# First transforms in four 64x64 tiles, x's rows spread over 128 partitions, and a new order of SP's transfers

## The chip, the cores and the metric

The kernel runs on one core of a Trainium2 chip. The metric is device microseconds (us) of one execution. Engines are named as the profile names them: PE (TensorE's matmuls), PEld (its weight loads), DVE (VectorE), ACT (ScalarE), POOL (GpSimd) and SP (SyncE, which here only issues transfers).

## What is computed

A spectral layer and two dense layers on a batch of two sequences, 3008 positions by 256 features, in float32:

```python
X = np.fft.rfft(x, axis=1)                   # x: (2, 3008, 256)
Yr = Xr @ w_r - Xi @ w_i + b_r               # 256 x 256, complex
Yi = Xr @ w_i + Xi @ w_r + b_i
Yr, Yi = soft_threshold(Yr, 0.01), soft_threshold(Yi, 0.01)
y = np.fft.irfft(Yr + 1j * Yi, n=3008, axis=1)
h = y.reshape(6016, 256) @ w_in1             # to 2048, leaky slope alpha, back to 256
z = leaky(h, alpha) @ w_out1
out = smooth_relu(z @ w_in2) @ w_out2        # the same shapes again
```

## The kernel before

The transform of length 3008 is split as 47 x 64. The work comes in this order.

- **f1**, the first transform, along 47 points. `x` is prepared on the host as 16 groups (8 of each of the two batches) of 96 rows: 48 rows (47 and a row of zeros) of one half of the 64 points and 48 of the other, 4 KB a row. `load_x(g)` brings a group to partitions 0 to 95 of a tile of its own, `f1(g)` multiplies it with the 96x96 constant `c47` in four matmuls of 256 columns (float32, which the trace shows as two instructions each) into two banks, ACT copies one bank and DVE the other to the tile `ae`, and `store_a(g, h)` writes `ae` to DRAM: h=0 the rows for frequencies 0 to 11, from 48 partitions, h=1 those for 12 to 23 from the other 48.
- **f2**, the second transform, works on 24 items (12 of each batch), each two of the 24 frequencies k. `load_a(b, parts)` brings k ranges of the stored intermediate to the tile `a` of batch b with 128 partitions; `A_PARTS` are the pairs (first k, number of k). Item i reads k = 2i and 2i+1, a piece of the constants `m`, and later of `n` (`load_mn`).
- Behind f2 come `mix` (the complex 256x256 product with the weights `wm`), the threshold, `i1` (first inverse transform, its result `ve` stored to DRAM by `v_dr<-ve`, two items a transfer, through two buffers in turn), `load_v` and `p3` (the last transform: 48 rows on each half of the partitions, products of 64 rows by 64 columns on the four quarters of PE). The loop over items runs f2 of item j+2, mix of item j and i1 of item j-2 in turn, and beside them the conversion of the first dense layer's weights (`load_w` brings `u`; ACT begins each with the line that reads `u`).
- The two dense layers follow, from about 150 us to the end.

The order is written out by hand: engines run their instructions in the order of the code. Nearly all transfers are issued by SP, in one queue. SP's and ACT's transfers share eight completion semaphores in turn, so that a transfer also waits for the one that used its semaphore last. A transfer that must wait (for an evicted tile, or a store that it reads) holds up all behind it on SP. PE likewise waits in order: where f2 of an item has no data, nothing behind it runs.

Of the kernel before, what the change touches and what calls it, by code (L numbers as in the profile page):

```python
# [31 lines left out]
def fourier_constants():  # L32

    import numpy as np

    n1, k1 = np.arange(R1), np.arange(NK)
    a = 2 * np.pi * (np.outer(n1, k1) % R1) / R1

    c = np.zeros((2, 48, 2, 2, NK))
    for par in range(2):  # L40
        c[par, :R1, 0, par] = np.cos(a)
        c[par, :R1, 1, par] = -np.sin(a)
    c = c.reshape(96, 4, 2, NK // 2).transpose(0, 2, 1, 3).reshape(96, 96)
# [51 lines left out]
def spectral_mlp_kernel(ctx: ExitStack, tc: tile.TileContext, x, w_r, w_i, bias, c_f1, c_f2,  # L95
                        c_i1, c_i2, w_in1, w_out1, alpha, w_in2, w_out2, out):
    nc = tc.nc
    V, A, G, T = nc.vector, nc.scalar, nc.gpsimd, nc.tensor
# [3 lines left out]
    psum = ctx.enter_context(tc.tile_pool(name="psum", bufs=2, space=PSUM))  # L102
# [19 lines left out]
    def block(tag, shape, dtype, name):  # L122
        return base.tile(shape, dtype, tag=tag, name=name)
# [6 lines left out]
        p = block(f"p{npiece[0] % NP}", [128, 1024], F32R, name)  # L130
        return p[:, 112:112 + 768]

    a_dr = [[dram.tile([NT, 48, D], F32, name=f"a_dr{b}_{h}") for h in range(2)] for b in range(B)]
    v_dr = [dram.tile([96, NT, D], F32, name=f"v_dr{b}") for b in range(B)]


# [199 lines left out]
    def obank(shape, name, ahead=None):  # L336
# [14 lines left out]
    xs = {}

    def load_x(g):
        b, j = divmod(g, 8)
        tag = f"p{g}" if g < 6 else f"w{g - 6}" if g < 14 else f"c{g - 12}"
        xs[g] = block(tag, [96, 4, D], F32, f"x{b}_{j}")
        if g == 0:
            nc.sync.dma_start(xs[g][:, 0:1, :], x[b, j, :, 0:1, :])
            nc.sync.dma_start(xs[g][:, 1:4, :], x[b, j, :, 1:4, :])
        else:  # L360
            nc.sync.dma_start(xs[g], x[b, j])

    A_PARTS = ((0, 2), (2, 2), (4, 2), (6, 2), (8, 4), (12, 6), (18, 6))

    def load_a(b, parts):
        if a_sb[b] is None:
            a_sb[b] = block(f"a{b}", [128, NK, D], F32, f"a_{b}")
        for k, n in parts:
            h, k0 = divmod(k, NK // 2)
            src = a_dr[b][h].rearrange("t (q k) f -> (t q) k f", q=4)  # L370
            nc.sync.dma_start(a_sb[b][:, k:k + n, :], src[:, k0:k0 + n, :])

    def store_a(g, h):
        b, j = divmod(g, 8)
        nc.sync.dma_start(a_dr[b][h][4 * j:4 * j + 4].rearrange("t p f -> p t f"), aes[g][48 * h:48 * h + 48])

    def load_mn(k, tiles, src, h=None):

        s = slice(0, 8) if h is None else slice(4 * h, 4 * h + 4)
        nc.sync.dma_start(tiles[k][:, s, :].rearrange("p k f -> p (k f)"),  # L380
                          src[:, 1024 * k + 128 * s.start:1024 * k + 128 * s.stop])
# [3 lines left out]
    def f1(g):  # L385
        b, j = divmod(g, 8)
        if g < 10:
            ae = block(f"w{8 + g}" if g < 5 else f"m{1 + g}" if g < 8 else f"w{g - 8}", [96, 4, D], F32, f"ae{g}")
        else:
            if g == 10:  # L390
                late.append(block("a1", [96, 6, 4, D], F32, "ae_late"))
            ae = late[0][:, g - 10]
        aes[g] = ae
        for i in range(2):
            ps = psum.tile([96, 2, D], F32, tag="h" if i else "e", name=f"ps1_{b}_{j}_{i}")
            for u in range(2):
                T.matmul(ps[:, u, :], c47, xs[g][:, 2 * i + u, :], start=True, stop=True)
            if i == 0:
                A.activation(ae[:, 0:2, :], ps, AF.Copy)
            else:  # L400
                V.tensor_copy(ae[:, 2:4, :], ps)
# [16 lines left out]
    for g in range(8):  # L418
        f1(g)
        store_a(g, 0)  # L420
        load_x(8 + g)
        if g == 3:
            load_mn(0, m_t, c_f2, 0)
        if g in (1, 2):
            A.dma_start(wm32[g - 1], (w_r, w_i)[g - 1].rearrange("(c p) e -> p c e", p=128))
    load_a(0, A_PARTS[:2])
    load_mn(0, m_t, c_f2, 1)
    load_a(0, A_PARTS[2:5])
    load_mn(1, m_t, c_f2, 0)
    load_mn(0, n_t, c_i1, 0)  # L430
    for g in range(8):
        store_a(g, 1)
    load_mn(1, m_t, c_f2, 1)
    load_mn(0, n_t, c_i1, 1)
    load_a(0, A_PARTS[5:])
    load_mn(1, n_t, c_i1)
    load_mn(2, m_t, c_f2)
# [54 lines left out]
    def split_wm(k, w):  # L492
        hi, lo = (wm[k][:, z].rearrange("p c (h q) -> p c q h", h=2) for z in range(2))
        split(w.rearrange("p c (q h) -> p c q h", h=2), hi, lo, A)

    for g in range(8, 16):
        f1(g)
        if g < 15:
            store_a(g, 0)
        if g == 8:  # L500
            T.matmul(ri[0].rearrange("p z e -> p (z e)"), ones, b_t[0:1].rearrange("p z e -> p (z e)"), start=True, stop=True)
            V.tensor_copy(b_t, ri[0])
        if g == 9:
            split_wm(0, wm32[0])
            V.scalar_tensor_tensor(ws[0], wm32[0], -1.0, wm32[1], op0=ALU.mult, op1=ALU.subtract)
        if g == 11:
            split_wm(1, ws[0])
            V.tensor_tensor(ws[1], wm32[1], wm32[0], op=ALU.subtract)
        if g == 13:
            split_wm(2, ws[1])  # L510
# [169 lines left out]
            ops[int(what[0])](what[1])  # L680
    for name in "HshLl":
        ops[2](name)
    store_a(15, 0)
    for j in range(n):
        parts = f2_parts(*items[j + 2]) if 0 < j < n - 2 else None
        if j + 1 < n:
            mix_sum(*items[j + 1])
        if parts is not None:
            parts_now(parts())
        mix(*items[j])  # L690
        if j >= 2:
            i1(*items[j - 2])

        if j == 3:
            for g in range(8, 16):
                store_a(g, 1)
        if j == 5:
            load_a(1, A_PARTS[:2])
        if j == 6:
            load_mn(2, n_t, c_i1, 0)  # L700
            load_a(1, A_PARTS[2:3])
            load_mn(2, n_t, c_i1, 1)
            load_a(1, A_PARTS[3:5])
# [384 lines left out]
```

## Time and profile before

| | |
|---|---|
| median of three runs | 1104.85 us (1102.56 to 1106.7) |
| the profiled execution | 1102.65 us, of which its span is 1100.6 us |
| PE busy in the span | 1087.2 us, 99% |
| TensorE's granted clock | 0.999 of full speed |
| moved by DMA | 101.19 MB, 92 GB/s over the span |

The span is that of the instructions; some 2 us of the execution lie outside it. A busy PE says little of what it waits for inside a matmul, so stretches are read one by one: the first 36 us hold f1, the stretch to about 150 us the items, the rest the dense layers. The DMA share of a stretch is the mean busy share of the core's 16 DMA engines; with the rate beside it one sees whether a full set of engines also moves many bytes.

### The profile page before, as it was taken

To read this page: it belongs to the slowest core of one execution; us is meant where nothing else is said; L and a number is where in the kernel's file an instruction comes from. 1 tells how busy PE (TensorE), PEld (TensorE's weight loads), DVE (VectorE), ACT (ScalarE), POOL (GpSimd) and SP (SyncE) were. 2 spreads that over 40 slices of the span, in tenths; PEclk is the share of its full clock that TensorE was granted. 3 is DMA by queue.
4 is the path that set the end of the run, shared out by engine and by line. 5 is a ranking of instruction groups with operands and counts; after the bars stand their busy time and mean duration, and the time that the engine had idled before them with its cause. 6 is when DMAs were issued, how large, how long until landed. Compare 5 with 4: busy or idle time off the path is not lost.

```text
span 1100.6 us, 17043 instructions
## 1 busy us (share of the span) xinstructions
PE 1087.2 (99%) x6368; PEld 955.7 (87%) x6368; DVE 897.4 (82%) x1572; ACT 815.9 (74%) x1499; POOL 36.9 (3%) x36
## 2 busy tenths in 40 slices
PE   9989999999999999999999999999999999999998
PEld 6878888888888998888889988888899888888897
DVE  3769759888879979989999877877878878878876
ACT  3557776656776768888888777877778878777876
POOL 0025400000000000000000000000000000000000
PEclk9999999999999999999999999999999999999999
DMA  9898754101322403324226720010010000100101
GB/s 265 299 277 261 204 142 108 39 1 67 126 97 97 171 20 115 115 96 141 89 97 248 273 90 1 1 39 1 1 38 1 37 1 1 39 1 1 39 1 37
DMA packets 49860, 101.19 MB, mean 92 GB/s; under 512 B 5009, under 2 KB 27249, under 8 KB 49778
## 3 DMA queue, kind: packets, MB, share of 16 engines
q1 hardware_dynamic: 48832, 99.41, 27.6%
q8 instruction: 50, 0.82, 0.3%
q10 hardware_dynamic: 946, 0.69, 0.2%
q14 instruction: 32, 0.26, 0.1%
HBM read 64.57 MB, written 35.52 MB: 91 GB/s over the span
## 4 chain that ended last, share of the span: by engine, by line
PE 82%; ACT 3%; DVE 2%; issue 0%; ACTq 0%; DVEq 0%
PE pq L114 10%; PE pq L115 10%; PE pq L116 10%; PE seeded L114 4%; PE seeded L116 4%; PE seeded L115 4%; PE psh L114 4%; PE pso L114 4%; PE psh L116 4%; PE psh L115 4%; PE pso L116 4%; PE pso L115 4%; PE psA L114 3%; PE psA L116 3%; PE psA L115 3%; PE psC L116 3%
## 5 line engine op out<-in xcount | busy, mean ns | idle before, releaser
L114 PE MATMUL pq<-gh,w 128*128 128x512 f32 (+1 forms) x576 | 216.6, 376 | 1.0 <-ACT yt L874 1.0
L115 PE MATMUL pq<-gl,w 128*128 128x512 f32 (+1 forms) x576 | 216.0, 375 | 0.4 <-DVE gl L845 0.2
L116 PE MATMUL pq<-gh,w 128*128 128x512 f32 (+1 forms) x576 | 215.8, 375 | 0.0
L842 ACT ACTIVATE gh<-ta 128x512 fp32r<-128x512 f32 (+1 forms) x144 | 88.0, 619 | 92.1 <-DVE ta L839 85.9
L641 ACT ACTIVATE ta<-psh,slopes 128x512 f32<-128x512 f32 (+1 forms) x96 | 65.1, 678 | 78.7 <-DVE ta L643 42.3
L114 PEld LDWEIGHTS pq<-gh,w 128*128 128x128 f32 x576 | 108.8, 189 | 15.9 <-ACT yt L874 3.1
L115 PEld LDWEIGHTS pq<-gl,w 128*128 128x128 f32 x576 | 108.9, 189 | 13.7 <-DVE gl L845 1.0
L116 PEld LDWEIGHTS pq<-gh,w 128*128 128x128 f32 x576 | 108.9, 189 | 12.8
L845 DVE TENSOR_TENSOR gl<-tb,gh 128x512 fp32r<-128x512 f32 (+1 forms) x96 | 65.3, 680 | 60.8 <-ACT gh L842 60.7
L845 DVE TENSOR_TENSOR gl<-ta,gh 128x512 fp32r<-128x512 f32 (+1 forms) x144 | 97.3, 676 | 3.1 <-ACT gh L842 1.4
L111 DVE TENSOR_TENSOR gl<-ta,gh 128x512 fp32r<-128x512 f32 (+1 forms) x96 | 65.2, 679 | 37.9 <-ACT gh L108 37.5
L933 DVE TENSOR_TENSOR h<-psC,s 128x512 f32<-128x512 f32 (+1 forms) x72 | 48.8, 678 | 40.8 <-PE psC L116 34.1
L114 PE MATMUL psh<-mxh,w 128*128 128x512 f32 (+1 forms) x192 | 72.2, 376 | 0.1
L114 PE MATMUL pso<-gh,w 128*128 128x512 f32 (+1 forms) x192 | 72.3, 377 | 0.0
L116 PE MATMUL pso<-gh,w 128*128 128x512 f32 (+1 forms) x192 | 71.9, 375 | 0.0
L115 PE MATMUL psh<-mxl,w 128*128 128x512 f32 (+1 forms) x192 | 71.9, 375 | 0.0
L116 PE MATMUL psh<-mxh,w 128*128 128x512 f32 (+1 forms) x192 | 71.9, 375 | 0.0
L115 PE MATMUL pso<-gl,w 128*128 128x512 f32 (+1 forms) x192 | 71.9, 375 | 0.0
L643 DVE SCALAR_TENSOR_TENSOR ta<-psh,slopes,ta 128x512 f32<-128x512 f32 (+1 forms) x96 | 70.5, 734 | 0.0
L839 DVE SCALAR_TENSOR_TENSOR tb<-tb,h 128x512 f32<-128x512 f32 (+1 forms) x96 | 60.7, 673 | 0.0
L831 ACT ACTIVATE ta<-ta 128x512 f32<-128x512 f32 (+1 forms) x96 | 59.3, 617 | 1.6
L842 ACT ACTIVATE gh<-tb 128x512 fp32r<-128x512 f32 (+1 forms) x96 | 59.3, 618 | 0.0
(163 smaller groups left out, 2640.1 us busy)
## 6 DMA issues: line engine op xcount, KB each, us to landing
s<-kept SPq DMA_DIRECT2D x32, 512.0 KB, 4.3
u<-in_w_in SPq DMA_DIRECT2D x32, 256.0 KB, 3.0
u<-in_w_out SPq DMA_DIRECT2D x32, 256.0 KB, 3.3
kept<-sh SPq DMA_DIRECT2D x16, 512.0 KB, 2.9
kept<-wh SPq DMA_DIRECT2D x16, 512.0 KB, 2.7
w<-kept SPq DMA_DIRECT2D x16, 512.0 KB, 5.5
v_dr<-ve SPq DMA_DIRECT2D x12, 512.0 KB, 3.9
v<-v_dr SPq DMA_DIRECT2D x32, 192.0 KB, 5.3
```

What stands on the lines that cost most here:

```text
L111: V.tensor_tensor(lo, src, hi.bitcast(F32), op=ALU.subtract)
L114: T.matmul(ps, wl, xh, start=start, stop=False, skip_group_check=chained)
L115: T.matmul(ps, wh, xl, start=False, stop=False, skip_group_check=chained)
L116: T.matmul(ps, wh, xh, start=False, stop=stop, skip_group_check=chained)
L641: A.activation(ta, ps, AF.Copy, scale=slope[:, f:f + 1])
L643: V.scalar_tensor_tensor(ta, ps, sign[:, f:f + 1], ta, op0=ALU.mult, op1=ALU.max)
L831: A.activation(self.t, self.t, AF.Square)
L839: V.scalar_tensor_tensor(self.t, self.t, 1.0, self.h, op0=ALU.min, op1=ALU.max)
L842: A.activation(halves(self.gh, self.m), like_halves(self.t, self.m), AF.Copy)
L845: V.tensor_tensor(halves(self.gl, self.m), like_halves(self.t, self.m), halves(self.gh, self.m).bitcast(F32), op=ALU.subtract)
L933: V.tensor_tensor(blk.h, ps[x], ps[y_], op=ALU.add)
```

## The change

Four things are changed.

- A group of x is 64 rows and 32 rows, brought by two transfers: the 64 to the even partitions, the 32 to every fourth partition from 1 on. The other 32 partitions hold zeros, which a memset of every x tile at the start writes (POOL 14 of them, DVE three; the first tile is shared). A load of x waits for the memset of its tile.
- `f1` is four matmuls of 64 rows by 64 columns by 512, one on each quarter of PE, and the two banks that they fill have 128 partitions. The frequencies 0 to 7 come out on every fourth partition, 8 to 23 on every second one.
- `store_a` h=0 now writes 8 frequencies from 32 partitions, h=1 16 frequencies from 64. `load_a` fetches each part in two transfers, one for each half of the partitions.
- SP's order: h=1 of batch 0 is stored ahead of part (8, 4), which now needs it; all stores of batch 1 stand ahead of the second weight tile instead of between items; some one-off operations of DVE and PE move by a group.

```diff
-    c = np.zeros((2, 48, 2, 2, NK))
...
-    c = c.reshape(96, 4, 2, NK // 2).transpose(0, 2, 1, 3).reshape(96, 96)
+    c = np.zeros((2, 64, 64))
+    rows = np.array([2 * i if i < 32 else 4 * (i - 32) + 1 for i in range(R1)])
+    c[:, rows[:, None], 4 * np.arange(16)] = cs[:, :, :8].reshape(R1, 16)
+    c[:, rows[:, None], 2 * np.arange(32) + 1] = cs[:, :, 8:].reshape(R1, 32)
...
-    a_dr = [[dram.tile([NT, 48, D], F32, name=f"a_dr{b}_{h}") for h in range(2)] for b in range(B)]
+    a_dr = [[dram.tile([8, 4, 2, (16, 32)[h], D], F32, name=f"a_dr{b}_{h}") for h in range(2)] for b in range(B)]
...
+    for g in range(16):
+        tag = f"p{g}" if g < 6 else f"w{g - 6}" if g < 14 else f"c{g - 12}"
+        xs.append(block(tag, [128, 4, D], F32, f"x{g}"))
+    V.memset(xs[0][:, 0:2], 0.0)
+    G.memset(xs[0][:, 2:4], 0.0)
     warm = rot.tile([128, 512], F32, tag="ta", name="warm")
     V.memset(warm, 0.0)
+    for g in range(1, 16):
+        (V if g in (3, 6) else G).memset(xs[g], 0.0)
...
-        if g == 0:
-            nc.sync.dma_start(xs[g][:, 0:1, :], x[b, j, :, 0:1, :])
-            nc.sync.dma_start(xs[g][:, 1:4, :], x[b, j, :, 1:4, :])
-        else:
-            nc.sync.dma_start(xs[g], x[b, j])
+        nc.sync.dma_start(xs[g][0:128:2], x[b, j, 0:64])
+        nc.sync.dma_start(xs[g][1:128:4], x[b, j, 64:96])
...
-            h, k0 = divmod(k, NK // 2)
-            src = a_dr[b][h].rearrange("t (q k) f -> (t q) k f", q=4)
-            nc.sync.dma_start(a_sb[b][:, k:k + n, :], src[:, k0:k0 + n, :])
+            h = k >= 8
+            src = a_dr[b][h].rearrange("j w q (z k) f -> z (j w q) k f", z=2)
+            for z in range(2):
+                nc.sync.dma_start(a_sb[b][64 * z:64 * z + 64, k:k + n, :], src[z][:, k - 8 * h:k - 8 * h + n])
...
-        nc.sync.dma_start(a_dr[b][h][4 * j:4 * j + 4].rearrange("t p f -> p t f"), aes[g][48 * h:48 * h + 48])
+        nc.sync.dma_start(a_dr[b][h][j].rearrange("w q i f -> (q i) w f"),
+                          aes[g][h:128:4 - 2 * h].rearrange("p s r f -> p (s r) f"))
...
-        for i in range(2):
-            ps = psum.tile([96, 2, D], F32, tag="h" if i else "e", name=f"ps1_{b}_{j}_{i}")
-            for u in range(2):
-                T.matmul(ps[:, u, :], c47, xs[g][:, 2 * i + u, :], start=True, stop=True)
...
+        ps = [psum.tile([128, 2, D], F32, tag="eh"[r], name=f"ps1_{b}_{j}_{r}") for r in range(2)]
+        for q in range(2):
+            for r in range(2):
+                rows = slice(64 * r, 64 * r + 64)
+                T.matmul(ps[r][64 * q:64 * q + 64], c47[rows, :], xs[g][rows, q:4:2, :], start=True, stop=True)
+        A.activation(ae[:, :, 0], ps[0], AF.Copy)
+        V.tensor_copy(ae[:, :, 1], ps[1])
...
-    load_a(0, A_PARTS[2:5])
+    load_a(0, A_PARTS[2:4])
     load_mn(1, m_t, c_f2, 0)
     load_mn(0, n_t, c_i1, 0)
     for g in range(8):
         store_a(g, 1)
+    load_a(0, A_PARTS[4:5])
+    load_mn(0, n_t, c_i1, 1)
     load_mn(1, m_t, c_f2, 1)
-    load_mn(0, n_t, c_i1, 1)
...
     for g in range(8, 16):
         f1(g)
-        if g < 15:
-            store_a(g, 0)
...
+        store_a(g, 0)
+        store_a(g, 1)
...
-        if j == 3:
-            for g in range(8, 16):
-                store_a(g, 1)
```

SP's queue in the second half of f1, where a store of one group stands ahead of the load of another (`x1_1` before and `x9` after are the same group). Before:

```order
L375 DMA a_dr0_0_68<-ae0_114 48x4x256
L361 DMA x1_0_124<-in_x 96x1024
L375 DMA a_dr0_0_68<-ae1_126 48x4x256
L361 DMA x1_1_136<-in_x 96x1024
L375 DMA a_dr0_0_68<-ae2_139 48x4x256
```

After:

```order
L379 DMA a_dr0_0_68<-ae0_146 32x4x256
L363 DMA x8_85<-in_x 64x1024
L364 DMA x8_85<-in_x 32x1024
L379 DMA a_dr0_0_68<-ae1_158 32x4x256
L363 DMA x9_86<-in_x 64x1024
L364 DMA x9_86<-in_x 32x1024
L379 DMA a_dr0_0_68<-ae2_171 32x4x256
```

Three transfers a group instead of two, with a smaller store and the same bytes of x.

SP's queue from the last x load to the load of the part (8, 4) of the tile `a_0`. Before, that part is the 128x1024 row, ahead of the stores of h=1 (`a_dr0_1`):

```order
L361 DMA x1_7_211<-in_x 96x1024
L371 DMA a_0_213<-a_dr0_0_68 128x512 x2
L380 DMA m0_100<-in_c_f2 128x512
L371 DMA a_0_213<-a_dr0_0_68 128x512 x2
L371 DMA a_0_213<-a_dr0_0_68 128x1024
L380 DMA m1_101<-in_c_f2 128x512
L380 DMA n0_103<-in_c_i1 128x512
L375 DMA a_dr0_1_69<-ae0_114 48x4x256
```

After, eight transfers of 64 partitions carry the first four parts (four of them and a piece of `m0` stand ahead of this excerpt), and the eight stores of h=1 come ahead of part (8, 4), the last row:

```order
L375 DMA a_0_247<-a_dr0_0_68 64x512 x4
L385 DMA m1_133<-in_c_f2 128x512
L385 DMA n0_135<-in_c_i1 128x512
L379 DMA a_dr0_1_69<-ae0_146 64x4x256
L379 DMA a_dr0_1_69<-ae1_158 64x4x256
L379 DMA a_dr0_1_69<-ae2_171 64x4x256
L379 DMA a_dr0_1_69<-ae3_184 64x4x256
L379 DMA a_dr0_1_69<-ae4_197 64x4x256
L379 DMA a_dr0_1_69<-ae5_209 64x4x256
L379 DMA a_dr0_1_69<-ae6_223 64x4x256
L379 DMA a_dr0_1_69<-ae7_235 64x4x256
L375 DMA a_0_247<-a_dr0_1_69 64x1024 x2
```

Item 4 is the first to read part (8, 4); it now stands behind 2.1 MB of stores.

## Rows read from the trace of the kernel before

**Rows 1.** The page, busy time of each engine.

```profile
PE 1087.2 (99%) x6368; PEld 955.7 (87%) x6368; DVE 897.4 (82%) x1572; ACT 815.9 (74%) x1499; POOL 36.9 (3%) x36
```

**Rows 2.** Windows: length, busy us (instructions) of PE, PEld, DVE, ACT, POOL; clock, DMA share, GB/s.

```profile
0.00:36.00 36.00, 34.25 (x141) 23.37 (x142) 16.37 (x24) 13.76 (x20) 0.20 (x4) 1.00 0.90 259
65.00:84.00 19.00, 15.23 (x122) 13.23 (x123) 13.54 (x27) 11.28 (x28) 5.89 (x5) 1.00 0.92 294
```

**Rows 3.** Windows: x loads; loads of 128 partitions; v loads, half the partitions each.

```profile
8.00:12.00 4.00, 4.00 (x20) 3.05 (x19) 1.60 (x3) 1.33 (x3) 0.00 (x0) 1.00 1.03 262
50.00:54.00 4.00, 4.00 (x35) 3.50 (x34) 2.65 (x5) 2.31 (x7) 0.00 (x0) 1.00 0.99 406
160.00:168.00 8.00, 8.00 (x39) 7.01 (x38) 7.12 (x12) 6.80 (x11) 0.00 (x0) 1.00 1.04 209
```

**Rows 4.** Timeline of PE: the end of f1, then f2 of items 0 and 4.

```profile
27.98 7.17 PE L397 MATMUL ps<-x,c 96*96 96x256 f32 x32 [0.26 <-DMA x<-in_x]
35.19 1.16 PE L448 MATMUL psf<-m,a 128*128 128x128 f32 x8
...
44.99 1.06 PE L448 MATMUL psf<-m,a 128*128 128x128 f32 x8
```

**Rows 5.** Timeline of PE: the start of f1, right behind the warming matmuls.

```profile
5.03 3.34 PE L397 MATMUL ps<-x,c 96*96 96x256 f32 x12
```

**Rows 6.** Groups by line: DVE's memset, and POOL's one-input operation.

```profile
L343 DVE MEMSET warm<- 128x512 f32 x1 | 0.5, 485 | 0.9 <-PEq L1076 0.9
...
L193 POOL TENSOR_SCALAR cm<-cm 128x512 f32<-128x512 f32 x8 | 6.1, 768 | 62.8 <-DMA a_dr<-ae_late 62.8
```

**Rows 7.** Timeline of PE: one p3 on PE's four quarters, then f2.

```profile
111.71 1.15 PE L613 MATMUL ps<-slopes,v 48*64 48x47 f32 x64
112.79 1.16 PE L448 MATMUL psf<-m,a 128*128 128x128 f32 x8
```

**Rows 8.** Instructions on x: SP's issues, ns min/median/max.

```profile
L361 SPq DMA_DIRECT2D x<-in_x x15: 312/423/602, 1.6 to 26.2; - x15
```

**Rows 9.** SP's waits, 0 to 36 us: total, times, longest.

```profile
SPq L361 <- DMA wm<-in_w_r: 5.1, 1, 5.1
```

**Rows 10.** Timeline of SP: issues of a, m, v_dr and u.

```profile
31.98 2.02 SPq L371 DMA_DIRECT2D a<-a_dr  x2
...
35.94 0.43 SPq L380 DMA_DIRECT2D m<-in_c_f  x1
...
64.64 0.38 SPq L551 DMA_DIRECT2D v_dr<-ve  x1
...
75.66 0.47 SPq L149 DMA_DIRECT2D u<-in_w_out  x1
```

**Rows 11.** Issues in short windows at 35.9, 64.6, 75.5 and 183.6 us: us to landing.

```profile
m<-in_c_f SPq DMA_DIRECT2D x1, 256.0 KB, 6.9
...
v_dr<-ve SPq DMA_DIRECT2D x1, 512.0 KB, 4.6
...
u<-in_w_out SPq DMA_DIRECT2D x1, 256.0 KB, 4.3
...
u<-in_w_in SPq DMA_DIRECT2D x1, 256.0 KB, 3.0
```

**Rows 12.** Waits of the engines, 64 to 84 us: total, times, longest.

```profile
ACT ve L548 <- DMA v_dr<-ve: 3.3, 1, 3.3
ACT cm L163 <- DMA u<-in_w_out: 2.6, 1, 2.6
...
PE psf L448 <- ACT fh L471: 1.7, 1, 1.7
PE psf L448 <- DVE fl L469: 1.3, 1, 1.3
...
PE psi L544 <- ACT ve L548: 0.7, 1, 0.7
```

**Rows 13.** Timeline of ACT: the eviction that waited for v_dr's store.

```profile
69.33 0.66 ACT L548 ACTIVATE ve<-psi 128x256 f32<-128x256 f32 x2 [3.35 <-DMA v_dr<-ve]
```

More of the change, by code (lines that the diff above doesn't have):

```diff
@@ L37, in fourier_constants @@
     a = 2 * np.pi * (np.outer(n1, k1) % R1) / R1
-    c = np.zeros((2, 48, 2, 2, NK))
-    for par in range(2):
-        c[par, :R1, 0, par] = np.cos(a)
-        c[par, :R1, 1, par] = -np.sin(a)
-    c = c.reshape(96, 4, 2, NK // 2).transpose(0, 2, 1, 3).reshape(96, 96)
+    cs = np.stack([np.cos(a), -np.sin(a)], axis=1)
+    c = np.zeros((2, 64, 64))
+    rows = np.array([2 * i if i < 32 else 4 * (i - 32) + 1 for i in range(R1)])
+    c[:, rows[:, None], 4 * np.arange(16)] = cs[:, :, :8].reshape(R1, 16)
+    c[:, rows[:, None], 2 * np.arange(32) + 1] = cs[:, :, 8:].reshape(R1, 32)
+    c = c.reshape(128, 64)
     g = np.zeros((2, 64, 64))
@@ L340, in obank @@
         return psum.tile(shape, F32, tag=f"o{k}", bufs=1, name=name)
+    c47 = block("u2", [128, 1024], F32, "c47")[:, 0:64]
+    A.dma_start(c47, c_f1)
+    xs = []
+    for g in range(16):
[3 more added lines that the diff above has]
+    G.memset(xs[0][:, 2:4], 0.0)
     warm = rot.tile([128, 512], F32, tag="ta", name="warm")
     V.memset(warm, 0.0)
+    for g in range(1, 16):
+        (V if g in (3, 6) else G).memset(xs[g], 0.0)
     ri = [psum.tile([128, 2, D], F32, tag=f"o{k}", bufs=1, name=f"ri{k}") for k in range(2)]
@@ L387, in f1 @@
         if g < 10:
-            ae = block(f"w{8 + g}" if g < 5 else f"m{1 + g}" if g < 8 else f"w{g - 8}", [96, 4, D], F32, f"ae{g}")
+            ae = block(f"w{8 + g}" if g < 5 else f"m{1 + g}" if g < 8 else f"w{g - 8}", [128, 2, 2, D], F32, f"ae{g}")
         else:
             if g == 10:
-                late.append(block("a1", [96, 6, 4, D], F32, "ae_late"))
+                late.append(block("a1", [128, 6, 2, 2, D], F32, "ae_late"))
             ae = late[0][:, g - 10]
         aes[g] = ae
-        for i in range(2):
-            ps = psum.tile([96, 2, D], F32, tag="h" if i else "e", name=f"ps1_{b}_{j}_{i}")
-            for u in range(2):
-                T.matmul(ps[:, u, :], c47, xs[g][:, 2 * i + u, :], start=True, stop=True)
[L398 to L401, printed above, removed]
+        ps = [psum.tile([128, 2, D], F32, tag="eh"[r], name=f"ps1_{b}_{j}_{r}") for r in range(2)]
[5 more added lines that the diff above has]
+        V.tensor_copy(ae[:, :, 1], ps[1])
     late = []
@@ L423, in spectral_mlp_kernel @@
             load_mn(0, m_t, c_f2, 0)
+        if g == 5:
+            T.matmul(ri[0].rearrange("p z e -> p (z e)"), ones, b_t[0:1].rearrange("p z e -> p (z e)"), start=True, stop=True)
+            V.tensor_copy(b_t, ri[0])
         if g in (1, 2):
@@ L497, in spectral_mlp_kernel @@
         f1(g)
-        if g < 15:
-            store_a(g, 0)
-        if g == 8:
-            T.matmul(ri[0].rearrange("p z e -> p (z e)"), ones, b_t[0:1].rearrange("p z e -> p (z e)"), start=True, stop=True)
-            V.tensor_copy(b_t, ri[0])
+        store_a(g, 0)
+        store_a(g, 1)
         if g == 9:
             split_wm(0, wm32[0])
+        if g == 10:
             V.scalar_tensor_tensor(ws[0], wm32[0], -1.0, wm32[1], op0=ALU.mult, op1=ALU.subtract)
@@ L507, in spectral_mlp_kernel @@
             split_wm(1, ws[0])
+        if g == 12:
             V.tensor_tensor(ws[1], wm32[1], wm32[0], op=ALU.subtract)
@@ L682, in spectral_mlp_kernel @@
         ops[2](name)
-    store_a(15, 0)
     for j in range(n):
@@ L1066 @@
     xp[:, :, :, :R1] = x.reshape(B, R1, 2, NT // 4, 4, D).transpose(0, 3, 2, 1, 4, 5)
+    xp = np.concatenate([xp[:, :, :, k].reshape(B, NT // 4, -1, 4, D) for k in (slice(0, 32), slice(32, 48))], axis=2)
     c_f1, c_f2, c_i1, c_i2 = fourier_constants()
     arrays = {
-        "x": xp.reshape(B, NT // 4, 96, 4, D), "w_r": w_r, "w_i": w_i, "bias": np.stack([b_r, b_i])[None],
+        "x": xp, "w_r": w_r, "w_i": w_i, "bias": np.stack([b_r, b_i])[None],
         "c_f1": c_f1, "c_f2": c_f2, "c_i1": c_i1, "c_i2": c_i2,
```

6 lines of the change are left out of this document (1 added, 5 removed).

## The prediction

> **What bounds the kernel now.** The page comes first: PE is busy for 99% of the span [rows 1], so over the whole kernel a DMA or a copy costs nothing unless PE stands for it, and time can only be won where PE stands, or works longer than it must. The windows by stage come next [rows 2]: over the first 36 us, which hold f1, the DMA engines are 90% busy at 259 GB/s, so that stage is close to two limits at once; from 65 to 84 us PE stands for 3.77 of 19 us. The third view is the rates of three kinds of load with the DMA engines full [rows 3]: x loads, on partitions 0 to 95, move 262 GB/s; loads of 128 partitions 406; v loads, each on 48 rows of one half of the partitions, 209. The reader should see a busy share near 1 in all three rows and rates that differ by two. Last come PE's timeline, where f1 runs without a gap and f2 of item 0 starts at 35.19 us [rows 4], and the waits between 64 and 84 us [rows 12].
>
> **The change, step by step.** Unit prices from these rows: a group of x (393 KB) takes 1.50 us of the queue now and 0.97 at 406 GB/s; 262 KB takes 0.65; a 131 KB transfer to half the partitions 0.63 at 209 GB/s, and 0.32 at 406. A lone 262 KB load lands 3.0 us after its issue [rows 11], 2.35 more than it moves: I put 1.7 of that ahead of the data and 0.65 behind. SP issues a transfer in 0.42 us [rows 8].
>
> *The memsets.* POOL's memset of 1024 columns has no row. From below it is twice DVE's 485 ns for 512, 0.97 us; from above twice POOL's 768 ns for an operation that also reads, 1.54 [rows 6]. At 1.25 x15's tile is zeroed at 0.45 + 0.6 + 13 x 1.25 = 17.3 us (21 at the upper end), before SP comes to it; the first eight groups run at about the memsets' own pace, and I charge nothing. DVE's extra memset moves the warming matmuls, and with them the start of f1, from 5.03 [rows 5] to 5.5 us.
>
> *f1 on PE.* Before, a group is 8 instructions in 1.8 us (32 in 7.17 [rows 4]). After, it is 8 instructions of 512 columns. A p3, which uses the four quarters in the same order, issues 64 instructions of 47 columns in 1.08 us [rows 7]; at f1's 216 ns for 256 columns they would take 2.5 one after the other, so at least 2.3 run at once. A group takes 0.86 us if four do, 1.5 if 2.3 do. f1 alone would end between 19 and 30 us; I take 1.0.
>
> *The x loads.* Up to x15 the queue carries 6.29 MB of x, 1.05 of stores (h=0), 0.26 of m and 0.52 of wm. x in the strided rows has no row of its own: 406 GB/s from above, 209 from below. It reaches all partitions in even steps, half of each transfer in either half, like the 128-partition loads, so I take 406. Then 8.12 MB take 20.0 us from 3.1 on. SP now stands 5.1 us for the first wm transfer [rows 9]: the ninth x load shares its semaphore, and it does so after too; with shorter queues I leave 1.8 us. x15 lands at 25.5, f1 of it ends at 26.5, the two halves of the first part of `a` take 2 x 0.63, and f2 of item 0 starts at 27.3 instead of 35.19: 7.9 us ahead.
>
> *Part (8, 4).* Item 4's f2 follows item 0's by 9.8 us [rows 4], so it would be ready at 37.1. Its data stands behind, from 25.5 on: eight half loads (5.0 us), three pieces of m and n (1.95), eight stores of 262 KB (5.2). The last store lands at 37.7; part (8, 4) can be issued only then, and takes 2.35 + 0.4 + 2 x 1.25: it lands at 43.0. Such loads run worse than their bytes: between 31.98 us and 42.8 five loads of `a` and two of m landed [rows 10, 11], 10.8 us for 2.1 MB, which by price is 5.2 + 2.35. Of these 3.3 us I allow 1.5. Item 4 starts at 44.5 instead of 44.99. PE stands some 7 us for it, and of the 7.9 us ahead 0.5 are left. PE's pace in f1 doesn't enter: f1 may end 6 us later at the same sum.
>
> *What is late next.* Before, the ACT eviction of item 4's i1 waits 3.35 us, ready at 65.98, for the first v_dr store, which lands at 69.24 [rows 10, 11, 13], 24.25 us behind item 4's f2; PE loses 1.3 + 0.7 by it [rows 12]. After, between part (8, 4) and that store the queue carries: n and m 1.3, the other k of `a` (1.57 MB in halves) 7.5, n and m 2.6, u 1.3, the 16 stores of batch 1 7.75, u 1.3, the store 1.3: 23.05 us, so 1.2 of the 2.0 are saved. The third u then lands another 1.3 + 2.5 + 1.3 later, 28.2 us behind item 4's f2, against 35.0 (79.96 less 44.99) before. ACT waited 2.6 us for it and PE lost 1.7 [rows 10, 11, 12]: saved. Beyond, half loads of batch 1 cost 7.8 us more of the queue, with parts issued ten or more us before their items; nothing. The DVE and PE operations moved by a group lie in f1, where both have idle time.
>
> *Sum.* 0.5 + 1.2 + 1.7 = 3.4 us saved, against a profiled execution of 1102.65 us (span 1100.6 and 2 us around it): 1099.2. The median of the runs is 2.2 above that execution, which would make 1101.4; I forecast **1100.5**.
>
> **A rule weighed against the rows.** The row says that a load into one half runs at 209 GB/s, and v loads, which take the two halves in turn, gain nothing by turns. The Trainium skill, *DMA: Bandwidth & Descriptors*, section *Rules for kernel authors*, says the same against this change: two transfers to the two halves serialize, and one of 128 partitions should be used. The trace agrees (209 against 406), which is why the fast rival below has less than a quarter.
>
> **The rivals.**
>
> *The halves of `a` overlap (0.22).* The two z transfers are neighbours in the queue; if they run as one at 406 GB/s, item 0 starts at 27.0, part (8, 4) lands at 40.8 with the same allowance, 4.2 ahead, the store of v_dr comes 19.5 us behind item 4 and the whole 2.0 + 1.7 is saved: 7.9 us, 1096. Against it stand the v loads.
>
> *The fuller half sets x's time (0.20).* Before, 262 KB of a group go to the lower half: 1.25 us at 209 GB/s, measured 1.50, a fifth more. After, each half gets 197 KB: 0.94, with the same fifth 1.13 us a group. That is 16 x 0.16 = 2.6 us later: 0.8 saved, 1103. By the Trainium skill, *SBUF — State Buffer*, section *Door 1: The DMA port swizzle*, bits 2 to 4 and bit 6 of a partition's number pick its port; I count 8 rows on the fullest port before and 6 after, and 1.50 x 6/8 is an estimate of 1.13 too.
>
> *x stays at 1.50 us a group (0.12).* Then the wait for wm is hidden and x15 comes 8.5 - 1.8 = 6.7 us later: 3.3 lost, 1107. The change then doesn't do what it says.
>
> *Slower: each strided transfer runs like a half (0.10).* If the 16 DMA engines meet on one half at a time, x runs at 209 GB/s, 1.88 us a group: 14.6 - 1.8 = 12.8 us later, 9.4 lost, 1113. For it speaks that 96 partitions already run nearer to 209 than to 406. The loss passes 0.5% from 1.65 us a group on, 238 GB/s.
>
> **How the numbers follow.** The forecast has 0.36, its own range 1097 to 1104 from the allowance (0 to 3.3 us) and the 2.2 us between execution and median. Half of the fast case lies over 1094.5, and the loss at 1.50 us a group under 1109: 1094.5 to 1109 leaves out about 2 in 10. About 0.5%, 5.5 us, is what a measurement of this kernel can tell from no change. Faster: nearly all of the fast case and a quarter of the forecast, 0.31. Slower: the last rival and a quarter of the one before, 0.13. Same: 0.56.
>
> **What would show it.** In the changed profile: x loads at 350 to 406 GB/s between 6 and 10 us; x15 landed near 25.5 us; f2 of item 0 near 27; PE standing 5 to 7 us before f2 of item 4, released by `a`; half loads near 209 GB/s; the ACT wait for `u` gone, and that for v_dr's store shorter. Wrong would be: x at 262 GB/s or less, memsets over 1.6 us that hold the loads, or item 4 not waiting for its data.

## The result: slower by 0.7%

The changed kernel's median is 1112.34 us (six runs, 1110.46 to 1116.47), that of the kernel before on the same chip 1105.09 (six runs): a recorded ratio of 1.0073, 95% interval 1.0049 to 1.0098 (the quotient of the two medians is 1.0066; all ratios below are the recorded ones). The forecast was 1100.5, the range 1094.5 to 1109.

The profiled execution has a span of 1111.0 us against 1100.6. These 10.4 us are more than the 7.3 between the medians, because the profiled execution of before lies 2.4 us under its median and this one near its own. From the page of the changed kernel: the span, PE's busy time (against [rows 1]), and in 40 slices of 27.8 us the clock and the DMA share.

```profile
span 1111.0 us, 17135 instructions
...
PE 1081.9 (97%) x6368; PEld 942.8 (85%) x6368; DVE 899.7 (81%) x1575; ACT 815.7 (73%) x1499; POOL 49.0 (4%) x50
...
PEclk9789999999999999999999999999999999999999
DMA  7799747100233403223326740010010000100100
```

PE works 5.3 us less and the span is 10.4 longer: it stands about 16 us more. The loss lies in the first slices, where the granted clock is down as well. The windows there (columns as in [rows 2]):

```profile
4.50:9.00 4.50, 3.34 (x22) 0.67 (x24) 1.38 (x2) 1.19 (x2) 4.50 (x6) 1.00 0.92 280
13.50:31.60 18.10, 11.40 (x70) 2.75 (x74) 8.27 (x12) 6.14 (x9) 0.00 (x0) 0.84 0.79 249
36.00:50.00 14.00, 12.73 (x82) 10.61 (x82) 8.24 (x20) 5.82 (x13) 0.00 (x0) 0.76 0.88 275
50.00:57.70 7.70, 0.08 (x1) 0.01 (x1) 1.85 (x4) 0.90 (x2) 0.00 (x0) 0.69 0.63 172
57.70:63.20 5.50, 5.48 (x26) 5.50 (x26) 1.95 (x4) 1.29 (x3) 0.00 (x0) 0.50 1.02 243
...
58.00:66.20 8.20, 8.20 (x49) 7.70 (x49) 2.64 (x5) 3.02 (x8) 0.00 (x0) 0.68 1.00 244
64.00:84.00 20.00, 20.00 (x167) 17.68 (x164) 13.55 (x26) 13.13 (x32) 1.55 (x2) 1.00 1.00 323
```

Read the second row first. While x is loaded, from 13.5 to 31.6 us, the DMA engines are 79% busy at 249 GB/s: data does not set the pace. SP does, as its timeline shows (start and length; each issue but the first starts 0.04 to 0.12 us behind the end of the one before):

```profile
13.53 0.47 SPq L364 DMA_DIRECT2D x<-in_x  x1
14.10 0.54 SPq L363 DMA_DIRECT2D x<-in_x  x1
14.68 0.59 SPq L364 DMA_DIRECT2D x<-in_x  x1
15.39 0.67 SPq L379 DMA_DIRECT2D a_dr<-ae  x1
16.16 0.54 SPq L363 DMA_DIRECT2D x<-in_x  x1
16.75 0.59 SPq L364 DMA_DIRECT2D x<-in_x  x1
17.45 0.64 SPq L379 DMA_DIRECT2D a_dr<-ae  x1
18.17 0.55 SPq L363 DMA_DIRECT2D x<-in_x  x1
```

A group is three issues, and from 16.16 to 18.17 that takes 2.01 us. Instructions on the tiles of x (ns min/median/max), against [rows 8]:

```profile
L363 SPq DMA_DIRECT2D x<-in_x x16: 473/552/593, 1.5 to 31.0; - x16
L364 SPq DMA_DIRECT2D x<-in_x x16: 474/590/620, 2.1 to 31.6; - x16
L355 POOL MEMSET x<- x13: 951/952/955, 1.2 to 11.8; 128x1024 f32 x13
```

One issue took 423 ns and brought a whole group; now two take 552 and 590. Ahead of this stretch SP stood for the first wm transfer (waits from 8 to 14 us, total, times, longest):

```profile
SPq L364 <- DMA wm<-in_w_r: 3.8, 1, 3.8
```

The last x transfer is issued at 31.6 and lands at 36.3 (32.9 before); f2 of item 0 starts at 39.1 (35.2). SP issues the eight h=1 stores from 42.05 to 48.4 and part (8, 4) only at 51.77:

```profile
42.05 6.35 SPq L379 DMA_DIRECT2D a_dr<-ae  x8
51.77 1.14 SPq L375 DMA_DIRECT2D a<-a_dr  x2
```

PE's timeline shows the rest, item 1's last products and item 4's f2 (against [rows 4]):

```profile
49.69 0.39 PE L494 MATMUL ri<-wm,fl 128*128 128x256 f32 x2
57.72 2.04 PE L456 MATMUL psf<-m,a 128*128 128x128 f32 x8 [7.64 <-DMA a<-a_dr]
...
64.47 1.16 PE L456 MATMUL psf<-m,a 128*128 128x128 f32 x8
```

PE stands 7.64 us for part (8, 4) of `a`, which is issued when the last h=1 store has landed (issued at 47.7, 4.1 us to landing). Then the same f2 that takes 1.16 us at 64.47 takes 2.04: from 57.7 to 63.2 the granted clock is 0.50, that is 1.2 GHz. Item 5 follows item 4 by 6.8 us instead of some 4.15. From 64 to 84 us, where PE lost 3.77 us before [rows 2], it now loses nothing.

So item 4's f2 starts 12.7 us later, the lower clock costs some 2.6 behind it, 3.8 us of stalls are gone, and f2 of the last item starts 11.1 later (144.9 against 133.8).

### The profile page after: what moved, and what is told of

Same layout as the page of the kernel before. It is cut to its first block, busy times and chain, and to the rows that moved or that the text cites. A ratio compares the mean times of both kernels' runs of the same rounds, so it can differ in the third digit from the quotient of the medians.

```text
span 1111.0 us, 17135 instructions
## 1 busy us (share of the span) xinstructions
PE 1081.9 (97%) x6368; PEld 942.8 (85%) x6368; DVE 899.7 (81%) x1575; ACT 815.7 (73%) x1499; POOL 49.0 (4%) x50
## 3 DMA queue, kind: packets, MB, share of 16 engines
q1 hardware_dynamic: 49200, 99.41, 27.8%
## 4 chain that ended last, share of the span: by engine, by line
PE 81%; ACT 2%; DVE 2%; issue 1%; ACTq 0%; DVEq 0%
PE pq L116 10%; PE pq L117 10%; PE pq L118 10%; PE seeded L116 4%; PE seeded L118 4%; PE seeded L117 4%; PE psh L116 4%; PE pso L116 4%; PE psh L117 4%; PE psh L118 4%; PE pso L117 3%; PE pso L118 3%; PE psA L116 3%; PE psA L118 3%; PE psA L117 3%; PE psC L118 3%
## 5 line engine op out<-in xcount | busy, mean ns | idle before, releaser
L116 PE MATMUL psh<-mxh,w 128*128 128x512 f32 (+1 forms) x192 | 72.2, 376 | 0.1
L117 PE MATMUL pso<-gl,w 128*128 128x512 f32 (+1 forms) x192 | 71.9, 375 | 0.0
L118 PE MATMUL pso<-gh,w 128*128 128x512 f32 (+1 forms) x192 | 71.9, 375 | 0.0
L118 PE MATMUL psh<-mxh,w 128*128 128x512 f32 (+1 forms) x192 | 71.9, 375 | 0.0
L117 PE MATMUL psh<-mxl,w 128*128 128x512 f32 (+1 forms) x192 | 71.9, 375 | 0.0
```

The source lines that it names most:

```text
L116: T.matmul(ps, wl, xh, start=start, stop=False, skip_group_check=chained)
L117: T.matmul(ps, wh, xl, start=False, stop=False, skip_group_check=chained)
L118: T.matmul(ps, wh, xh, start=False, stop=stop, skip_group_check=chained)
```

## The experiments

The first theory was that SP's issues set the pace of x (the issue theory); the rival, that x's strided rows move slowly (the data theory). In the table x15 is the last group of x. Later runs ask what holds part (8, 4), what the clock costs, and whether the losses add up. All times in us from the trace; ratios to the kernel before on the same chip.

| kernel | x15 landed | item 4's f2 | first v_dr store landed | item 10's f2 | last item's f2 | ratio (interval) |
|---|---|---|---|---|---|---|
| before | 32.9 | 45.0 | 69.2 | 72.5 | 133.8 | 1 |
| changed | 36.3 | 57.7 | 82.0 | 85.4 | 144.9 | 1.0073 (1.0049 to 1.0098) |
| e1 padded x, one transfer | 29.6 | 50.5 | 76.0 | 79.3 | 138.8 | 1.0039 (1.0024 to 1.0054) |
| e2 h=1 stores on ACT | 40.1 | 55.5 | 77.6 | 81.0 | 140.5 | 1.0077 (1.0049 to 1.0104) |
| e3 wm later | 34.6 | 54.5 | 79.1 | 82.4 | 141.9 | 1.0075 (1.0051 to 1.0098) |
| e4 matmuls in the stand | 36.6 | 56.4 | 81.5 | 84.8 | 147.5 | 1.0105 (1.0081 to 1.0129) |
| e5 half of x's issues on ACT | 29.8 | 51.1 | 76.6 | 79.8 | 139.3 | 1.0051 (1.0036 to 1.0066) |
| e6 `a` joined, two pieces | 35.4 | 79.3 | - | 132.4 | 240.9 | 1.0974 (1.0956 to 1.0992) |
| e7 e4, v_dr on ACT | 35.8 | 56.7 | - | 87.7 | 151.2 | 1.0141 (1.0125 to 1.0157) |
| e8 e1, e3, e6, v_dr on ACT | - | 74.5 | - | 126.7 | 235.3 | 1.0925 (1.0909 to 1.0942) |
| e9 `a` joined, even rows | 35.7 | 52.1 | 76.8 | 80.0 | 139.5 | 1.0053 (1.0036 to 1.0071) |
| e10 e1, e3, e9 | 31.4 | 48.6 | 72.2 | 76.2 | 135.7 | 1.0007 (0.9997 to 1.0016) |
| e11 e10, e2 | 35.3 | 47.0 | 66.2 | 71.9 | 131.4 | 0.9974 (0.9965 to 0.9984) |
| e12 e10, stores back | 31.9 | 48.9 | 66.0 | 76.5 | 136.0 | 1.0003 (0.9993 to 1.0012) |

(A dash: the trace has no landing there.)

**e1: x padded in DRAM, one transfer a group.** It brings 128 rows, 32 of them zero; the memsets are gone with it.

```diff
-        nc.sync.dma_start(xs[g][0:128:2], x[b, j, 0:64])
-        nc.sync.dma_start(xs[g][1:128:4], x[b, j, 64:96])
+        nc.sync.dma_start(xs[g], x[b, j])
```

> x stands in DRAM with its zero rows, so a group is one transfer of 128 rows (524 KB) and the memsets of x are gone. Issue theory: in the changed kernel SP sets the pace, with three strided transfers a group in 2.03 us (0.60, 0.70 and 0.72 from one issue to the next) after its stand of 3.8 us. With two a group (about 0.45 and 0.7) the data sets it: 0.52 and 0.13 MB at 406 GB/s are 1.62 us a group, x15 lands near 29 us instead of 36.3, item 4's f2 comes near 50.5 instead of 57.7, the time is 1104 to 1106. Data theory: strided or not, x moves at the 241 GB/s at which its groups landed in the first 12 us (1.63 us a group of 393 KB); then 524 KB take 2.2 us, x15 lands no earlier than 36, the time is 1112 to 1117.

The window of 4.5 to 9 us:

```profile
4.50:9.00 4.50, 4.07 (x33) 0.95 (x32) 2.00 (x3) 1.79 (x3) 0.00 (x0) 1.00 1.02 412
```

A third more bytes land 6.7 us sooner, at 412 GB/s against 280. x15 and item 4 come where the issue theory had them; the time, 1107.15, is above its 1104 to 1106. This run changes the shape of the transfers too, so e5 had to part the two theories.

**e2: the eight h=1 stores of batch 0 issued by ACT**, at the same place of the code (`store_a(g, 1, A)`).

> The eight h=1 stores of batch 0 are issued by ACT's queue behind f1 of group 7, not by SP behind the first parts of a. Issue theory: the DMA engines have a fifth of their time free in f1, so the 2.1 MB cost x at most 1 to 2 us; part (8, 4) is issued at 42 to 44 instead of 51.8 and lands at 47 to 49, and PE, ready at 49.9, stands 0 to 2 us for item 4 instead of 7.9; with the clock's share back the time is 1102 to 1105. Data theory: the 2.1 MB push x15 back by their whole 5.2 us, item 0's f2 to 44, and item 4's f2 to 55 or later: 1108 to 1112.

Each theory was right in part, and the data theory's numbers came nearer: 1110.85 us, item 4 at 55.5. PE hardly stands for item 4 any more, but x15 lands 3.8 us later and item 0's f2 starts at 43.0: while x is loaded the changed kernel's engines have a fifth of their time free, not room for 2.1 MB. The last item is 4.4 us ahead of the changed kernel in the trace; the timed runs do not tell the two apart.

**e3: the wm loads behind groups 6 and 7 of f1** (`if g in (6, 7)`).

> The two wm loads are issued by ACT behind f1 of groups 6 and 7 instead of 1 and 2; nothing else. If SP's stand of 3.8 us for the first wm transfer (9.7 to 13.5) is lost time of an SP that is the bound, most of it comes back: x15 lands near 33, item 4's f2 near 54.5, time 1108 to 1110, as long as no other transfer of SP's stands for them. If the stand is covered by data still queued, nothing changes: x15 at 36, 1111 to 1113.

SP's stand is gone, x15 lands 1.7 us sooner rather than 3.3, item 4 comes at 54.5 as expected; the time, 1111.12, is above the expected 1108 to 1110. The last item is 3.0 ahead in the trace; again the timed runs do not separate it from the changed kernel.

**e4: PE kept busy in its stand.** The matmuls' result is not used.

```diff
+        if j == 2:
+            dummy = psum.tile([128, 512], F32, tag="o3", bufs=1, name="dummy")
+            for _ in range(30):
+                T.matmul(dummy, wm[0][:, 0, 0, 0:128], wm[0][:, 1].rearrange("p c e -> p (c e)"), start=True, stop=True)
         parts = f2_parts(*items[j + 2]) if 0 < j < n - 2 else None
```

> 30 matmuls of 512 columns on data already there, into a free bank, between item 1's mix and item 4's f2; they keep PE busy for some 6.5 of the 7.9 us in which it stood, and their result is read by no one. Clock theory: after the stand the granted clock was at the lower level until 63.2, matmul starts 213 ns apart against 112, which cost 2.7 us; with PE busy up to item 4's f2 that is gone: 1109 to 1110, with f2 of item 4 still near 57.7. If the clock costs nothing in the end (its loss taken back at a later wait), the time stays at 1111 to 1113.

PE's timeline: the added matmuls (28 of 30 are recorded), item 4's f2, now 1.13 us, and its first products, at the full clock:

```profile
48.81 6.53 PE L694 MATMUL dummy<-wm 128*128 128x512 f32 x28
56.40 1.13 PE L456 MATMUL psf<-m,a 128*128 128x128 f32 x8 [1.06 <-DMA a<-a_dr]
57.29 0.69 PE L494 MATMUL psk<-wm,fh 128*128 128x256 f32 x4
```

Item 5 follows by 4.1 us instead of 6.8: the clock's price is confirmed. But the time, 1114.71, is above both expectations; the ratio is, if anything, higher than the changed kernel's. Of ACT's waits from 62 to 93 us the largest that a transfer ends:

```profile
ACT ve L555 <- DMA v_dr<-ve: 4.4, 1, 4.4
```

The first v_dr store lands at 81.5, as in the changed kernel (82.0), and the eviction that reuses its buffer waits for it. Item 9 still comes 3.9 us ahead of the changed kernel; item 10 is only 0.6 ahead, and PE, idle again, goes on at the lower clock (item 11 follows item 10 by 6.6 us). That gave the next theory: in before, the changed kernel and e1 to e4, item 10's f2 starts 3.3 to 3.4 us behind this landing.

**e5: the second transfer of x issued by ACT**, nothing else (`A.dma_start(xs[g][1:128:4], ...)`).

> The second of the two x transfers of each group (32 rows) is issued by ACT's queue; same transfers, same bytes, same rows. Issue theory: SP has two issues a group instead of three (0.61 and 0.73 us, 1.34 instead of 2.03), the data at 406 GB/s about 1.3; from the stand for wm on that saves up to 0.65 us for each of the last six or seven groups: x15 lands at 32 to 33 instead of 36.3, item 4's f2 comes near 54, the first v_dr store lands near 78 instead of 82.0, item 10's f2 3.3 us behind it, and the time is 1.002 to 1.005 of the kernel before, where the changed kernel has 1.0073. Data theory: nothing moves, x15 at 36, ratio 1.006 to 1.008.

```profile
4.50:9.00 4.50, 3.78 (x18) 0.70 (x16) 1.31 (x2) 0.00 (x0) 4.50 (x6) 1.00 0.97 351
13.50:29.00 15.50, 14.94 (x99) 4.30 (x91) 9.59 (x14) 8.29 (x13) 0.00 (x0) 0.88 0.95 307
```

The same transfers, the same bytes, the same rows: 351 GB/s against 280 early, and x15 lands 6.5 us sooner (3 to 4 were expected; the ratio is just over the expected 1.005). Strided rows can move faster than they did, against the data theory, and the issue theory holds in the main. Three things stay open. One: behind its own x issues ACT comes to the wm loads later (start of the first in the changed kernel and in e5):

```profile
8.01 0.42 ACTq L432 DMA_DIRECT2D wm<-in_w_r  x1
...
13.57 0.52 ACTq L432 DMA_DIRECT2D wm<-in_w_r  x1
```

SP does not stand for wm here, as in e3. So the shared issues by themselves are worth less than 6.5 us: against e3, which has no such stand either, x15 lands 4.8 us sooner. Two: the transfers get a second queue together with a second issuer, and no run parts the two; for the issue speaks SP's row with hardly a gap. Three: early the DMA share hardly rises, from 0.92 to 0.97, while the rate rises by a quarter, so a high share did not mean that data set the pace.

Under *Perfetto Trace Analysis*, section *DMA Optimizations*, the Trainium skill says that balancing transfers across the issuing engines may help where the making of descriptors is the bottleneck and the issuing engine looks busy. The trace agrees (351 against 280 GB/s).

**e6: each part of `a` as one transfer to 128 partitions**, its source still in two pieces (real and imaginary).

```diff
-            for z in range(2):
-                nc.sync.dma_start(a_sb[b][64 * z:64 * z + 64, k:k + n, :], src[z][:, k - 8 * h:k - 8 * h + n])
+            nc.sync.dma_start(a_sb[b][:, k:k + n, :], src[:, :, k - 8 * h:k - 8 * h + n])
```

> Each part of a is one transfer to 128 partitions instead of two to 64. Half-load theory (two halves one after the other at some 209 GB/s, and an issue of 0.64 us for each): four parts ahead of item 0 and the m and n save 2.4 us, part (8, 4) 1.2, the two parts of six 3.6: item 4's f2 at 54 instead of 57.7, the first v_dr store lands near 75 instead of 82.0, ratio 1.003 to 1.005. If the halves overlap already, the joined loads save only issues that are hidden: item 4 at 57, ratio 1.006 to 1.008.

A hundred us slower. From 39 to 49 us, while PE waits for these loads:

```profile
39.00:49.00 10.00, 3.06 (x12) 2.79 (x13) 0.85 (x2) 0.80 (x2) 0.00 (x0) 0.50 0.24 72
```

The DMA engines are 24% busy at 72 GB/s. Neither theory foresaw that, and the run says nothing on half loads.

**e7: e4, with the v_dr stores of batch 0 issued by ACT** right behind the evictions.

> e4's 30 matmuls before item 4's f2, and the v_dr stores of batch 0 issued by ACT right behind the eviction that fills them instead of by SP behind the stores of batch 1. In before, after and the four runs so far, item 10's f2 started 3.3 to 3.4 us behind the landing of the first v_dr store. Theory: that landing (82.0 after, 81.5 in e4) took the clock's gain back; the store now lands by 75, and item 10's f2 stands 24.9 us behind item 4's (six items of 4.15): near 81 instead of 85.4, ratio 1.003 to 1.005. Rival: what held in e4 was another wait (u, or PE's own work): item 10 again at 84 to 85, ratio 1.009 or more.

The rival's time, and worse. SP's, ACT's and PE's waits from 62 to 93 us:

```profile
SPq L379 <- DMA v_dr<-ve: 4.0, 1, 4.0
...
ACT cm L165 <- DMA u<-in_w_out: 6.3, 1, 6.3
PE psf L456 <- DVE fl L477: 5.5, 1, 5.5
```

The wait for v_dr is gone from ACT, but a store of batch 1 on SP shares the second v_dr store's semaphore and stands 4.0 us for it; all behind it is later, the second u among it (issued at 81.9 instead of 76.7 in e4), and ACT waits 6.3 us for that. So the landing of v_dr was one of two limits on ACT, and the stores of batch 1 on SP stand ahead of both.

**e8: padded x, later wm, e6's joined loads, v_dr on ACT.**

> Padded x in one transfer a group (e1), wm loads later (e3), parts of a in one transfer (e6) and v_dr stores on ACT (e7), without extra matmuls. If the queue ahead of part (8, 4) and of the v_dr store is all that the change lost: x15 lands at 27 to 29, item 4's f2 comes at 45 to 48, item 10's 25 us behind it, and the ratio is 0.997 to 1.001. If something else was lost too (PE's clock in f1, copies), 1.003 or more.

It has e6's loads and went the same way; it decides nothing.

**e9: e6 mended.** The constants' rows are put in the order (tile row, real or imaginary), so that a part's 128 rows lie at one even step.

```diff
-    m = m.reshape(8, 2, 2, 2, 2, NK, 2, R2).transpose(3, 0, 1, 4, 2, 5, 6, 7)
+    m = m.reshape(8, 2, 2, 2, 2, NK, 2, R2).transpose(0, 1, 4, 2, 3, 5, 6, 7)
...
+            src = a_dr[b][h].rearrange("j w q (z k) f -> (j w q z) k f", z=2)
+            nc.sync.dma_start(a_sb[b][:, k:k + n, :], src[:, k - 8 * h:k - 8 * h + n])
```

> e6 mended: the rows of c_f2 are ordered (tile row, real or imaginary), so a part of a is one transfer whose 128 rows lie at one even step in DRAM; e6's transfers, whose outermost step had two pieces, held the DMA engines 24% busy at 72 GB/s and say nothing on half loads. Half-load theory (two halves one after the other at some 209 GB/s, an issue of 0.64 us each): item 4's f2 at 54 instead of 57.7, the first v_dr store lands near 75 instead of 82.0, item 10's f2 at 81 to 82 instead of 85.4, ratio 1.003 to 1.005. If the halves overlapped already: item 4 at 57, ratio 1.006 to 1.008.

```profile
50.00:62.00 12.00, 9.92 (x70) 8.96 (x71) 5.14 (x10) 4.54 (x11) 0.00 (x0) 0.86 0.95 346
```

The stretch with the last two parts and the m, n and u around them moves 346 GB/s, where the stretch with the same parts in halves, and the end of an m ahead of them, moved 244 with the engines just as busy (58.0 to 66.2 us of the changed kernel). Item 4 comes 5.6 us sooner, 1.9 more than expected, item 10 follows v_dr's landing by 3.2; the ratio, 1.0053, is a little over the expected 1.003 to 1.005. Half loads are dear, and rather dearer than the prediction had them; each joined part also saves an issue, and the run doesn't part the two.

**e10: e1, e3 and e9 together.**

> e1 (padded x, one transfer a group), e3 (wm later) and e9 (a in one transfer) together. If the DMA queue ahead of part (8, 4) and of v_dr's store is all that the change lost, the gains add: x15 lands at 28, item 4's f2 comes near 45 to 47, v_dr's store lands near 66, item 10's f2 at 70 to 72 against 72.5 in the kernel before, ratio 0.997 to 1.001. If something else was lost, 1.002 or more.

Item 4 at 48.6 is just outside the expected 45 to 47, the ratio, 1.0007, just inside. The gains do not simply add: alone the three bring item 4 forward by 7.2, 3.2 and 5.6 us, together by 9.1, and x15, at 31.4, lands later than in e1. v_dr's store lands at 72.2 instead of 66 but no longer decides; item 10 is at 76.2 because item 5 follows item 4 by 6.8 us, at the lower clock behind a stand. PE's only wait from 38 to 93 us:

```profile
PE psf L450 <- DMA a<-a_dr: 4.7, 1, 4.7
```

**e11: e10, with e2's stores on ACT.**

> e10 and, as in e2, the eight h=1 stores of batch 0 issued by ACT behind f1 of group 7. Queue theory: their 2.1 MB move into f1's stage, which e1 has 88% busy, so x15 lands 2 to 4 us later than in e10, and part (8, 4) finds its data 6 us sooner; item 4's f2 at 43 to 46, PE hardly standing ahead of it, ratio 0.995 to 1.000. If ACT standing for semaphores holds its own evictions, item 0's f2 comes at 37 or later and the ratio is no better than e10's.

```profile
13.50:36.00 22.50, 11.41 (x74) 3.06 (x74) 8.53 (x14) 6.38 (x10) 0.00 (x0) 0.77 0.99 362
36.00:50.00 14.00, 13.53 (x114) 11.73 (x106) 12.69 (x27) 9.04 (x19) 0.00 (x0) 1.00 0.99 364
```

The engines are 99% busy at over 360 GB/s from 13.5 to 50 us, where the changed kernel moved 249 and 275. x15 lands 3.9 us later than in e10 and item 0's f2 starts at 37.7, later than in before, as the rival had it; yet item 4 starts at 47.0 with its data there, a little over the expected 43 to 46:

```profile
46.99 1.06 PE L450 MATMUL psf<-m,a 128*128 128x128 f32 x8
...
51.11 1.16 PE L450 MATMUL psf<-m,a 128*128 128x128 f32 x8
```

From there to the end of the items PE waits for no transfer, item 10 is 24.9 us behind item 4 and the last item 2.3 us ahead of before. The medians are 1100.44 against 1103.95 us, the ratio 0.9974: about 0.3% faster than the kernel before and 1% than the changed one.

**e12: e10, with batch 1's h=1 stores back between the items.**

> e10 with batch 1's h=1 stores put back to where the kernel before has them, between the items (one part of the change undone). Queue theory: 2.1 MB, 5.2 us, leave the queue ahead of v_dr's first store, which lands near 61 instead of 66; whether PE gains hangs on item 4: if item 4 with 25 us for six items sets item 10, nothing changes; if the store does, up to 2 us. Ratio 0.996 to 1.001.

v_dr's store lands 6.2 us sooner than in e10 (5 were expected), and nothing is won: in e10 item 4 and the lower clock behind it set item 10, not the store. In e10's order that part of the change costs nothing; in e4, where item 5 came without the lower clock, the same stores stood ahead of the v_dr store that PE lost time to.

## Why the prediction was wrong

**What failed: the x loads.** The prediction took the 8.12 MB up to x15 at 406 GB/s, 20.0 us, priced an issue at 0.42 us, the row of a transfer with one even step, and never set a group's issues against its data. At 0.42 three are 1.26 us, just under the 1.30 that the data take at 406 GB/s; at the 0.59 to 0.73 that these strided transfers take from one issue to the next they are 2.0. So x15 landed at 36.3 instead of 25.5, 10.8 us of the miss. The wait for wm was put at the ninth x load (in the trace of the kernel before it is the tenth, issued at 16.5), with 1.8 us uncovered; the semaphores are shared by transfers, not by groups, so it came at the fourteenth, in group 6, stood 3.8 and drained the queue: without it, in e3, x15 lands 1.7 sooner. With the issues shared as well, in e5, it lands another 4.8 sooner. And the strided rows reach 351 GB/s in e5 with the engines 97% busy, 1.12 us a group, not 0.97: an estimate of 2.4 us over 16 groups. With that rate and no stand the prediction's terms would give x15 at some 26.1 where e5 has 29.8; this rest of 3.7 us is not taken apart. (In e5 ACT's first evictions wait 10.6 us behind its x issues, and from 11.5 to 13.5 us the DMA engines are only 51% busy.) Of its signs, early x came between the two: 280 GB/s, under the 350 to 406 of the forecast and over the 262 that it called wrong. The figure of 1.12 meets the 1.13 that the prediction worked out from rows for its second rival. It had put the same 1.13, as an estimate, beside the Trainium skill, *SBUF — State Buffer*, section *Door 1: The DMA port swizzle*; the trace agrees (1.12), and no run here tests the ports otherwise.

**What held, later than forecast.** f1 on four quarters starts a group 0.86 us behind another at the full clock (its eight instructions of some 0.6 us each take 1.09 together), and was not the bound. A memset takes 0.95 us, just under the lower bound, and held SP little (waits of 0.4 us). Part (8, 4) was issued as the last store landed and PE stood 7.6 us for it (some 7 forecast). From x15's landing to item 4's f2 it took 21.4 us, 19.0 forecast: 2.4 us more. Over the bare sum of 17.5 that is 3.9, where the prediction had seen 3.3 in the kernel before and allowed 1.5. The row from 36.0 to 42.7 us below, with the eight half loads, has the DMA engines 72% busy at 190 GB/s while SP issues; the row behind it, with the stores, has them full at 354, where 406 was put. e9 shows half loads as dear as forecast or dearer. (The forecast start of item 0, 27.3, does not follow from its terms: 25.5 and twice 0.63 give 26.8. Only the length of PE's stand hangs on it.)

**What is late next.** v_dr's store landed 24.3 us behind item 4's f2, as far as before (24.25); 23.05 was forecast. PE lost hardly anything by it (item 10 follows item 9 by 4.31 us instead of 4.16, and ACT waits 1.0 for the store instead of 3.3), because item 5 had already lost time to the clock. The wait for `u` went as forecast. Of the 3.77 us of stalls 2.9 were to go; all went.

**What was left out: the clock.** Before, f1 kept PE busy and the clock full. Now f1's groups kept PE busy for only 11.4 of the 18.1 us from 13.5 to 31.6, and later PE stood 7.6 us; both times the granted clock fell to 0.50. The end of the first drop, and the stretch behind it up to the stand:

```profile
36.00:42.70 6.70, 5.55 (x25) 3.86 (x25) 1.53 (x4) 1.40 (x3) 0.00 (x0) 0.50 0.72 190
42.70:50.00 7.30, 7.18 (x60) 6.75 (x59) 6.70 (x17) 4.42 (x10) 0.00 (x0) 1.00 1.02 354
```

The first drop slowed the f2 of items 0 and 1, which cost nothing in the end, because item 4 had no data yet. The second slowed item 4 for 5.5 us of full work, which cost 2.6. e4 shows that price, and that winning it back alone gains nothing while v_dr's store is late.

**The rivals.** Three had x slower than the forecast. *The fuller half* had the price of the data right, 1.13 us a group against 1.12 in e5, and not the time: it left the issues out as well. Two had x much too slow. At 1.88 us a group one gave 1113, close to what was measured, and its bound held (a loss from 1.65 us a group on; 2.0 came). But its mechanism did not: the same rows moved 351 GB/s in e5, not 209, and the engines were idle a fifth of the time. The right number with the wrong cause would have led to the wrong mend. That *the halves of `a` overlap* is against e9, where joining them brought item 4 forward by 5.6 us.

## What to carry to other kernels

When a change cuts a transfer in two or gives it strided rows, price the issue by its shape and count, and set issues per group against data per group for each issuing queue; an issuing engine with hardly a gap is the sign. The DMA share beside it was 0.79 here while x and stores took turns, but 0.92 while SP issued x alone, so the share by itself does not tell. Spread the issues over two queues or make the rows one even step before asking for bandwidth. And follow a gain through the queue to the last wait it feeds: here e4's gain and e7's early store were both given back at the next transfer in line, while the same time taken out of the queue itself (e10, e11) reached the end.

## What the runs showed of the hardware

- SP's issues took, by median, 423 ns for 96 rows in one step, 432 for 128 in e1, 552 to 590 for strided or half-height loads, 636 for strided stores of h=0. The shape is not all: the 96 rows took 312 to 602 ns, and the 32 strided rows 477 when ACT issued them (e5). What else enters is open.
- A transfer whose outermost step has only two pieces leaves most DMA engines idle: 24% busy, 72 GB/s in e6, against 83% and 237 in the stretch with the same parts in e9 (33.9 to 41.0 us), where their 128 rows have one step. The Trainium skill, *DMA: Bandwidth & Descriptors*, section *Why a DMA increments its semaphore by 16 and not by 1*, says that the number of engines is the largest up to 16 that divides the outermost count of both sides; two here, as an estimate by that rule. The trace agrees in kind (24%, a piece of `m` included), though it doesn't show the engines apart.
- Behind a stand of 7.6 us PE worked from 57.7 to 63.2 us without a gap at the granted clock 0.50 (1.2 GHz) and then at 1.00 (2.4 GHz); behind one of 1.06 us (e4) it was at the full clock from the first matmul.
